# Scaling by the gates on VectorE and ScalarE, a unit's logits formed together, and another order of the first loads, in a fused attention and mixture-of-experts kernel

## The chip, the cores and the metric

One core of one Trainium2 chip runs the whole program. A time is the device time of one execution in microseconds (us). Five executions of the kernel before gave a median of 724.09 us (722.45 to 726.24). The engines are named as in the profile: PE is TensorE (PEld its weight loads), DVE is VectorE, ACT is ScalarE, POOL is GpSimd, SP is SyncE, which issues transfers here. A "q" behind a name (SPq, POOLq) is that engine's own queue of instructions.

## The reference

Sliding-window causal attention over 8 batches, 8 heads, 576 positions and a head size of 64 comes first, then a mixture of experts in which each of the 4608 tokens goes to one of eight experts. Both are f32.

```python
# attention: q, k, v of (8, 8, 576, 64), window 64
scores = scale * np.matmul(q, k.transpose(0, 1, 3, 2))
mask = (rel >= 0) & (rel < window)
scores = np.where(mask, scores, -1000000000.0)
scores = scores - np.max(scores, axis=-1, keepdims=True)
attn = np.exp(scores)
attn = attn / (np.sum(attn, axis=-1, keepdims=True) + 1e-09)
x = (attn @ v)            # laid out as (4608, 512)
# experts: w_gate (512, 8), w1 (8, 512, 1024), w2 (8, 1024, 512)
logits = x @ w_gate
expert_idx = np.argmax(logits, axis=1)
probs = np.exp(logits - logits.max(-1, keepdims=True))
probs /= probs.sum(-1, keepdims=True) + 1e-09
gate_w = probs[np.arange(N), expert_idx]
h = np.maximum(x_sorted[lo:hi] @ w1[e], 0.0)     # for each expert e
y_sorted[lo:hi] = h @ w2[e]
return gate_w[:, None] * y
```

The kernel multiplies x by its gate before the experts and not y after them, which is the same since the gate is positive.

## The kernel before, in words

**Units and steps.** Attention is cut into 16 units: four groups of two batches (`bg`), and in each group four pairs of heads (`g`). A unit is three steps (`c` = 0, 1, 2), so there are 48 steps, numbered `s`; each covers three blocks of 128 tokens. `step(s)` (lines 941 to 971) writes out one turn of a pipeline by hand, and every engine runs its own instructions strictly in that order. In step `s` these things are issued, in this order:

1. `scored(s + 1)`: 24 matmuls (line 628); `masked`, six DVE instructions that add the mask and take the row maximum (line 641); `softened`, six exponentials on ACT (line 651).
2. `weighted(s - 1)`: 24 matmuls with v (line 674) into the one bank 6.
3. `logit(s - 3)`: the matmuls with the gate's weights (line 711) from the transposed x of step `s - 3`.
4. `flipped(s)`: six PE transposes of the probabilities (line 659) into two banks of PSUM, copied out by DVE (first head) and ACT (second head), line 661.
5. `divided(s - 1)`: three DVE instructions (lines 684, 685, 688) that normalise and write x into a tile `xs`.
6. in the first step of a unit, the loads of v two units ahead and of q and k three units ahead, all on SP's queue; v also needs six POOL copies a unit (lines 567, 569, 573), which make a second, shifted copy `vb` of it.
7. `turned(s + 3)`: PE transposes of q and k for the next unit (eight, line 595, in the first two steps of a unit, two, line 587, in the third) and ACT copies.
8. `x_turned(s - 2)`: three PE transposes of x (line 699) and an ACT copy `xT` (line 702).
9. whatever `todo` holds for this step.

Steps 4, 7 and 8 and the small work of the routing take their PSUM banks in turn from one ring of four (`tr_ring`, banks 2 to 5). A step with all five uses comes back to its first bank with `x_turned`: those transposes wait until DVE has copied the first head of `flipped` out of that bank.

**Routing.** When the logits of a block of three tiles of a group are complete, `by_tokens` copies them out (ACT, line 722), transposes them in the next step (PE, line 725) and copies them back (DVE, line 726). After the third, `choose(bg)` works out expert, gate and rank in five parts, mostly small DVE instructions (lines 742 to 798). `after(s, ...)` (lines 878 to 900) spreads the parts over the following steps, then, tile by tile for nine tiles, `place` (two bf16 DVE instructions, line 802, that build the one-hot rows `lo`), `weigh` (x times its gate, 128x512 f32, in place) and `store` (the DMA of `xs` to `x_dram`, on POOL's queue). The groups' routing starts at steps 15, 27 and 39; the fourth group is dealt with after the last step. For groups 0 and 1 all nine `weigh` are on POOL (line 813). For group 2 seven are on POOL and two on ACT (line 811). In step 45 `first_tiles` forms `hi_e` on DVE (line 907) from the ranks, multiplies it with `lo` on PE (54 matmuls, line 914), and gathers the first tokens of expert 0. The matmuls of the experts follow from about 214 us.

**The first loads.** Before step -3 one queue, SP's, gets: q and k of unit 0 (eight DMAs of 128 KB), the gate's weights, a row of zeros for `x_dram`, the last 64 positions of q, k and v (six DMAs), v of unit 0 (four), q and k of unit 1 (eight), v of unit 1 (four), q and k of unit 2 (eight). A DMA further waits until the eighth DMA before it has landed, since eight semaphores go round.

Of the kernel before, what the change touches and what calls it, by code (L numbers as in the profile page):

```python
# [11 lines left out]
F32 = mybir.dt.float32  # L12
# [24 lines left out]
def kernel(  # L37
# [10 lines left out]
    nc = tc.nc  # L48
# [447 lines left out]
    with tc.manual_schedule(), ExitStack() as held, ExitStack() as brief:  # L496
# [2 lines left out]
        rp = held.enter_context(tc.tile_pool(name="rp", bufs=2))  # L499
        att = brief.enter_context(tc.tile_pool(name="att", bufs=2))  # L500
        xp = brief.enter_context(tc.tile_pool(name="xp", bufs=3))
        sc_ring, tr_ring = cycle((0, 1)), cycle((2, 3, 4, 5))


# [32 lines left out]
        def load_qk(u):  # L537
            bg, g = units[u]
            qks[u] = [qk_m(((u % 3 + 2) % 3 * 2 + n) * 1024, BG, NV, 2, D) for n in range(2)]
            for i in range(BG):  # L540
                for t, src in zip(qks[u], (q, k)):
                    for h in range(2):
                        nc.sync.dma_start(
                            out=t[:, i, :, h, :],
                            in_=src[bg * BG + i, 2 * g + h, 0:SM, :].rearrange("(p j) d -> p j d", j=NV),
                        )

        def load_rests(bg):

            at = 6144 + bg % 2 * 2048  # L550
            vr = qk_m(at + 1024, BG, H, D)
            rests[bg] = [qk_m(at, H, D), qk_m(at + 512, H, D), vr]
            for t, src in zip(rests[bg], (q, k)):
                for i in range(BG):
                    nc.sync.dma_start(
                        out=t[i * D : (i + 1) * D], in_=src[bg * BG + i, :, SM:S, :].rearrange("h p d -> p h d")
                    )
            for i in range(BG):
                nc.sync.dma_start(out=vr[D:P, i], in_=v[bg * BG + i, :, SM:S, :].rearrange("h p d -> p h d"))

        def load_v(u):
            bg, g = units[u]
            va, vb = v_ring[u % NVR]
            for i in range(BG):
                for h in range(2):
                    nc.sync.dma_start(out=va[:, i, :, h, 0:D], in_=whole(v, u, i, h))
                G.tensor_copy(out=vb[D:P, i, NV - 1, :, 0:D], in_=rests[bg][2][D:P, i, 2 * g : 2 * g + 2])

                nc.gpsimd.tensor_copy(  # L569
                    out=vb[0:D, i].rearrange("p j h d -> p (j h d)"),  # L570
                    in_=va[D:P, i].rearrange("p j h d -> p (j h d)"),
                )
# [141 lines left out]
                )  # L714
            return g == NG - 1

        def by_tokens(bg, c):

            if c == 0:
                logits_of[bg] = rp.tile([P, NTB, E], F32, name="logits")  # L720
            lgT = rp.tile([ST * GE, P], F32, name="lgT")
            nc.scalar.copy(out=lgT[:], in_=lgs[bg][:, c, :])
            yield
            tr = banks[next(tr_ring)](0, ST, P)
            nc.tensor.transpose(out=tr[:, 0, 0 : ST * GE], in_=lgT[:], identity=ident[0 : ST * GE, 0 : ST * GE])
            V.tensor_copy(
                out=logits_of[bg][:, c * ST : (c + 1) * ST, :],
                in_=tr[:, 0, 0 : ST * GE].rearrange("p (m e) -> p m e", e=GE)[:, :, 0:E],
            )

        last = B // BG - 1
# [187 lines left out]

        N = NU * NST  # L920
        load_qk(0)
        nc.sync.dma_start(out=wg[:, :, 0:E], in_=moe_w_gate.rearrange("(g p) e -> p g e", p=P))
        nc.sync.dma_start(out=x_dram[NT : NT + 1, :], in_=zrow[:])
        load_rests(0)
        load_v(0)
        load_qk(1)
        load_v(1)
        load_qk(2)

        for g in range(NG):  # L930
            step = NST * (g // 2) + g % 2 + 1
# [9 lines left out]
        def step(s):  # L941
            if 0 <= s + 1 < N:
                prs[s + 1] = softened(*masked(s + 1, scored(s + 1)))
            if 0 <= s - 1 < N:
                px = weighted(s - 1, pTs.pop(s - 1))
            ripe = 0 <= s - 3 < N and logit(s - 3)
            if 0 <= s < N:
                pTs[s] = flipped(prs.pop(s))
            if 0 <= s - 1 < N:
                divided(s - 1, px)  # L950
            if s >= 0 and s % NST == 0:
                u = s // NST
# [12 lines left out]
            if ripe:  # L965
                bg, c = (s - 3) // (NG * NST), (s - 3) % NST
                parts = by_tokens(bg, c)
                next(parts)
                todo.setdefault(s + 1, []).append(partial(next, parts, None))
                if c == NST - 1:  # L970
                    after(s + 1, choose(bg), bg)


        for n, s in enumerate((N - 6, N - 3)):
# [79 lines left out]
    with tc.manual_schedule():  # L1054
# [36 lines left out]

        def any_number():

            tiles_of = rt.tile([P, E, NTILE], F32, name="tiles_of")
            V.tensor_tensor(
                out=tiles_of[:], in0=_inner(cum[:], NTILE), in1=_ins(lane[:, 0:NTILE], 1, E), op=ALU.is_le
            )
            with nc.allow_low_precision("integers"):
                V.tensor_reduce(out=expert_i[:], in_=tiles_of[:].rearrange("p e t -> p t e"), axis=AX.X, op=ALU.add)
# [60 lines left out]
```

## Time and profile before

| | |
|---|---|
| median of five runs | 724.09 us (722.45 to 726.24) |
| the profiled execution: its own time | 719.12 us |
| its span | 717.4 us |
| its granted TensorE clock | 0.992 |
| PE, DVE, ACT, POOL busy | 687.2, 495.9, 258.6, 350.1 us |
| steps -3 to 47 and what follows to the first expert matmuls | 0 to about 215 us |
| `weigh` on POOL, 25 instructions | median 1562 ns |
| `weigh` on ACT, 11 instructions | median 708 ns |

The page has an overview, a list of groups of instructions with what ended the idle time before them, and further views: the timeline lists single instructions with start, duration and, in brackets, idle time before them and what ended it; the table of windows gives busy time per engine in stretches of the span. PE's busy time is modelled from pipelined matmuls, so a stretch in which PE is busy throughout can still be a slow one: the duration of a known bundle of matmuls tells which.

### The profile page before, as it was taken

The page shows a single profiled execution, that of the slowest core. Times are in us where ns is not written, and L with a number is a line of the kernel's source. Part 1 is how long each engine was busy: PE and PEld are TensorE (multiplying, and loading weights), DVE is VectorE, ACT ScalarE, POOL GpSimd, SP SyncE. Part 2 cuts the span into 40 slices and gives each one's busy share as a digit, 9 for nine tenths or more (in the row PEclk, how much of TensorE's full clock was granted, in tenths as well). Part 3 has the DMA queues.
Part 4 walks back from the last instruction along what each step waited for, and adds up shares of the span by engine and source line. Part 5 has one row for each costly group of instructions (what it writes and reads, how often), then busy time and mean ns, then how long its engine had stood idle before and what let it go on. Part 6 is the DMA issues. An engine that isn't in the chain of part 4 may idle for free. (4 is left out here: it accounts for less than half of the span.)

```text
span 717.4 us, 17946 instructions
## 1 busy us (share of the span) xinstructions
PE 687.2 (96%) x6882; PEld 605.8 (84%) x6882; DVE 495.9 (69%) x1636; ACT 258.6 (36%) x653; POOL 350.1 (49%) x360
## 2 busy tenths in 40 slices
PE   5999999999979999999999999999999999999993
PEld 3787888888769897897999999899889799889993
DVE  3576898898956768676776677568756677766731
ACT  4788888888745112101121111122110112111110
POOL 4223748569574117757452446645265745272001
PEclk9999999999999999999999999999999999999997
DMA  8998988989443364617102620640451710111000
GB/s 157 214 208 180 185 176 230 210 182 246 146 136 114 102 241 145 199 59 276 53 16 66 216 101 32 208 146 2 139 196 59 275 52 18 61 37 61 2 31 28
DMA packets 137288, 93.37 MB, mean 130 GB/s; under 512 B 117008, under 2 KB 117008, under 8 KB 137170
## 3 DMA queue, kind: packets, MB, share of 16 engines
q1 hardware_dynamic: 127858, 62.16, 32.5%
q0 software_dynamic: 8736, 27.53, 11.9%
q10 hardware_dynamic: 576, 2.10, 0.9%
q8 instruction: 74, 1.21, 0.7%
q14 instruction: 44, 0.36, 0.2%
HBM read 72.89 MB, written 20.45 MB: 130 GB/s over the span
## 5 line engine op out<-in xcount | busy, mean ns | idle before, releaser
L315 DVE STREAM_TRANSPOSE v_m<-qk_m 32x256 f32<-32x256 f32 x304 | 132.3, 435 | 7.9 <-DMA qk_m<-x_dram,at_g 2.3
L344 PE MATMUL bank<-qk_m,s 128*128 128x128 f32 x1024 | 122.5, 275 | 0.1
L344 PEld LDWEIGHTS bank<-qk_m,s 128*128 128x128 f32 x1024 | 118.3, 192 | 0.3 <-issue 0.3
L275 POOL DMA_INDIRECT qk_m<-x_dram,at_g x38 | 41.0, 1078 | 141.1 <-DVE v_m L315 112.7
L651 ACT ACTIVATE pr<-pr,mx 128x128 f32<-128x128 f32 x288 | 89.7, 390 | 32.6 <-DVE mx L641 32.3
L344 PE MATMUL bank<-qk_m,w 128*128 128x128 f32 x768 | 93.8, 275 | 0.7 <-PEq L1077 0.7
L344 PEld LDWEIGHTS bank<-qk_m,w 128*128 128x128 f32 x768 | 90.6, 192 | 4.2 <-issue 3.9
L295 POOL DMA_INDIRECT out_dram<-v_m,at_s x42 | 42.4, 1010 | 87.4 <-DVE v_m L384 85.2
L641 DVE CUSTOM_DVE_ANT_0 pr<-bank,mask 128x128 f32<-128x128 f32 x288 | 64.4, 286 | 29.0 <-PE bank L628 27.6
L384 DVE TENSOR_TENSOR v_m<-bank,v_m 128x256 f32<-128x256 f32 (+1 forms) x95 | 43.8, 480 | 44.9 <-PE bank L388 30.1
L569 POOL COPY v_m<-v_m 64x520 f32<-64x520 f32 x32 | 19.8, 619 | 69.1 <-DMA v_m<-in_v_dram 59.8
L140 POOL TENSOR_TENSOR s<-w 128x1024 f32<-128x1024 f32 x22 | 52.2, 2373 | 0.0
L674 PEld LDWEIGHTS bank<-v_m,pT 128*64 128x64 f32 x1152 | 40.8, 140 | 11.5 <-DVE xs L688 5.4
L674 PE MATMUL bank<-v_m,pT 128*64 128x65 f32 x1152 | 47.5, 230 | 2.5 <-DVE xs L688 2.4
L351 ACT COPY qk_m<-bank 128x512 f32<-128x512 f32 x16 | 9.4, 587 | 108.4 <-PE bank L344 70.2
L388 PE MATMUL bank<-qkT_m,v_m 128*128 128x256 f32 x216 | 48.3, 379 | 0.0
L628 PE MATMUL bank<-qkT_m 64*64 64x128 f32 x1152 | 45.6, 290 | 0.1
L388 PEld LDWEIGHTS bank<-qkT_m,v_m 128*128 128x128 f32 x216 | 41.0, 190 | 5.5
L595 PE MATMUL bank<-ident,qk_m 128*128 128x128 f32 x256 | 36.8, 287 | 8.3 <-DMA qk_m<-in_q_dram 7.5
L444 PEld LDWEIGHTS bank<-qk_m,w 128*128 128x128 f32 x320 | 43.9, 190 | 0.9 <-issue 0.7
L444 PE MATMUL bank<-qk_m,w 128*128 128x160 f32 x320 | 44.4, 299 | 0.4 <-ACT qk_m L327 0.4
L327 ACT COPY qk_m<-v_m 128x512 f32<-128x512 f32 x38 | 21.6, 615 | 58.6 <-DVE v_m L315 58.6
(174 smaller groups left out, 1248.0 us busy)
## 6 DMA issues: line engine op xcount, KB each, us to landing
w<-in_moe_w_dram SPq DMA_DIRECT2D x11, 2048.0 KB, 9.9
qk_m<-in_q_dram SPq DMA_DIRECT2D x72, 128.0 KB, 4.0
qk_m<-in_k_dram SPq DMA_DIRECT2D x72, 128.0 KB, 3.7
v_m<-in_v_dram SPq DMA_DIRECT2D x64, 128.0 KB, 4.2
qk_m<-in_moe_w_dram SPq DMA_DIRECT2D x3, 2048.0 KB, 10.9
x_dram<-xs POOLq DMA_DIRECT2D x6, 512.0 KB, 4.8
x_dram<-xs POOLq DMA_DIRECT2D x3, 768.0 KB, 5.1
w<-in_moe_w_dram ACTq DMA_DIRECT2D x4, 512.0 KB, 4.4
```

Of the source, the lines that this page charges most:

```text
L140: op()
L275: G.indirect_dma_start(out=xg[c], out_offset=None, in_=x_dram[:, :], in_offset=bass.IndirectOffsetOnAxis(ap=at_g[:, c : c + 1], axis=0),)
L295: put = G.indirect_dma_start(out=out[:, :], out_offset=bass.IndirectOffsetOnAxis(ap=at_s[:, c : c + 1], axis=0), in_=ys[c], in_offset=None ...
L315: V.transpose(out=xn[b * QD : (b + 1) * QD, :, :, a * QD : (a + 1) * QD].rearrange("p c g i -> p (c g) i"), in_=rows[a * QD : (a + 1) * QD ...
L344: nc.tensor.matmul(acc[:, f, :], lhsT=a[:, g, f * P : (f + 1) * P], rhs=b[:, g, :], start=(first and f == 0 and g == 0), stop=(g == HG - 1 ...
L384: plus = lambda out, a, b: V.tensor_tensor(out=out, in0=a, in1=b, op=ALU.add)
L388: nc.tensor.matmul(acc, lhsT=a[:, f, :], rhs=b[:, f, :], start=(start and f == 0), stop=(stop and f == HF - 1), skip_group_check=True,)
L444: nc.tensor.matmul(acc[:, i], lhsT=w1[:, g, f * P : (f + 1) * P], rhs=xq[:, g].rearrange("p c s -> p (c s)")[:, 0:HALF], start=(i + g == 0 ...
L628: nc.tensor.matmul(out_, lhsT=qT[rows, t, a * WINDOW : (a + 1) * WINDOW], rhs=rhs, start=True, stop=True, skip_group_check=True,)
L641: V.tensor_tensor_reduce(out=prs[h][:, m, :], in0=scs[h][:, m, :], in1=mask[:, m0 + m, :], scale=-scale, scalar=-2 * MASKED, op0=ALU.add, ...
L651: nc.scalar.activation(out=y, in_=y, func=AF.Exp, scale=-1.0, bias=mx[:, h, m : m + 1])
L674: nc.tensor.matmul(px[a * D : (a + 1) * D, h, m, :], lhsT=pTs[h][:, m, a * D : (a + 1) * D], rhs=vt[:, h, :], start=True, stop=True, skip_ ...
```

## The change

`weigh` leaves POOL. Groups 0 and 1 do all nine on DVE, one a step, at steps 4 to 12 after the routing's start; their `place` goes from 5 + 2m/3 to 5 + m, one a step. Group 2 does tiles 0, 1, 3 and 6 on ACT and five on DVE, some a step later than before. Stores stay on POOL's queue and follow the `weigh` of each third tile.

`logit` is called for all three steps of a unit at once, in the unit's third step, and `by_tokens` then moves three blocks in one ACT copy, three transposes into one bank, and one DVE copy. The fourth group keeps the form with single blocks.

Of the first loads, k of unit 0 and k's last positions go to ACT's queue. q and k of unit 1 come ahead of v of units 0 and 1; the gate's weights come behind these, the row of zeros last. A small buffer in a branch that these inputs don't take moves into another tile.

```diff
@@ load_qk / load_rests
-                for t, src in zip(qks[u], (q, k)):
+                for t, src, queue in zip(qks[u], (q, k), (nc.sync, nc.sync if u else nc.scalar)):
                     for h in range(2):
-                        nc.sync.dma_start(
+                        queue.dma_start(
...
-            for t, src in zip(rests[bg], (q, k)):
+            for t, src, queue in zip(rests[bg], (q, k), (nc.sync, nc.sync if bg else nc.scalar)):
@@ by_tokens
-        def by_tokens(bg, c):
+        def by_tokens(bg, c, n=1):
...
-            lgT = rp.tile([ST * GE, P], F32, name="lgT")
-            nc.scalar.copy(out=lgT[:], in_=lgs[bg][:, c, :])
+            lgT = (rp if n == 1 else lt).tile([ST * GE, n, P], F32, name=f"lgT{n}")
+            nc.scalar.copy(out=lgT[:], in_=lgs[bg][:, c : c + n, :])
             yield
-            tr = banks[next(tr_ring)](0, ST, P)
-            nc.tensor.transpose(out=tr[:, 0, 0 : ST * GE], in_=lgT[:], identity=ident[0 : ST * GE, 0 : ST * GE])
+            tr = banks[next(tr_ring)](0, n, ST * GE)
+            for i in range(n):
+                nc.tensor.transpose(out=tr[:, i], in_=lgT[:, i], identity=ident[0 : ST * GE, 0 : ST * GE])
@@ after
-                    do(5 + m * 2 // 3, partial(place, bg * NTB + m))
-                    do(5 + m * 2 // 3, partial(weigh, bg, m, G))
+                    do(5 + m, partial(place, bg * NTB + m))
+                    do(4 + m, partial(weigh, bg, m, V))
                     if m % ST == ST - 1:
-                        do(5 + m * 2 // 3, partial(store, bg, m // ST, G))
+                        do(4 + m, partial(store, bg, m // ST, G))
...
-                do((2, 2, 3, 3, 4, 4, 4, 5, 5)[m], partial(weigh, bg, m, nc.scalar if m in (2, 6) else G))
+                do((2, 3, 3, 4, 4, 4, 5, 5, 5)[m], partial(weigh, bg, m, nc.scalar if m in (0, 1, 3, 6) else V))
@@ first loads
         load_qk(0)
+        load_rests(0)
+        load_qk(1)
+        load_v(0)
+        load_v(1)
         nc.sync.dma_start(out=wg[:, :, 0:E], in_=moe_w_gate.rearrange("(g p) e -> p g e", p=P))
+        load_qk(2)
         nc.sync.dma_start(out=x_dram[NT : NT + 1, :], in_=zrow[:])
-        load_rests(0)
-        load_v(0)
-        load_qk(1)
-        load_v(1)
-        load_qk(2)
@@ step
-            ripe = 0 <= s - 3 < N and logit(s - 3)
+            ripe = 0 <= s - 3 < N and s % NST == NST - 1 and [logit(n) for n in range(s - 5, s - 2)][-1]
```

More of the change, by code (lines that the diff above doesn't have):

```diff
@@ L501 @@
         xp = brief.enter_context(tc.tile_pool(name="xp", bufs=3))
+        lt = brief.enter_context(tc.tile_pool(name="lt", bufs=1))
         sc_ring, tr_ring = cycle((0, 1)), cycle((2, 3, 4, 5))
@@ L552, in load_rests @@
             rests[bg] = [qk_m(at, H, D), qk_m(at + 512, H, D), vr]
-            for t, src in zip(rests[bg], (q, k)):
+            for t, src, queue in zip(rests[bg], (q, k), (nc.sync, nc.sync if bg else nc.scalar)):
                 for i in range(BG):
-                    nc.sync.dma_start(
+                    queue.dma_start(
                         out=t[i * D : (i + 1) * D], in_=src[bg * BG + i, :, SM:S, :].rearrange("h p d -> p h d")
@@ L715, in logit @@
             return g == NG - 1
-        def by_tokens(bg, c):
+        def by_tokens(bg, c, n=1):
             if c == 0:
                 logits_of[bg] = rp.tile([P, NTB, E], F32, name="logits")
-            lgT = rp.tile([ST * GE, P], F32, name="lgT")
-            nc.scalar.copy(out=lgT[:], in_=lgs[bg][:, c, :])
+            lgT = (rp if n == 1 else lt).tile([ST * GE, n, P], F32, name=f"lgT{n}")
+            nc.scalar.copy(out=lgT[:], in_=lgs[bg][:, c : c + n, :])
             yield
-            tr = banks[next(tr_ring)](0, ST, P)
-            nc.tensor.transpose(out=tr[:, 0, 0 : ST * GE], in_=lgT[:], identity=ident[0 : ST * GE, 0 : ST * GE])
+            tr = banks[next(tr_ring)](0, n, ST * GE)
+            for i in range(n):
+                nc.tensor.transpose(out=tr[:, i], in_=lgT[:, i], identity=ident[0 : ST * GE, 0 : ST * GE])
             V.tensor_copy(
-                out=logits_of[bg][:, c * ST : (c + 1) * ST, :],
-                in_=tr[:, 0, 0 : ST * GE].rearrange("p (m e) -> p m e", e=GE)[:, :, 0:E],
+                out=logits_of[bg][:, c * ST : (c + n) * ST, :],
+                in_=tr.rearrange("p n me -> p (n me)").rearrange("p (m e) -> p m e", e=GE)[:, :, 0:E],
             )
@@ L965, in step @@
             if ripe:
-                bg, c = (s - 3) // (NG * NST), (s - 3) % NST
-                parts = by_tokens(bg, c)
+                bg = (s - 3) // (NG * NST)
+                parts = by_tokens(bg, 0, NST)
                 next(parts)
                 todo.setdefault(s + 1, []).append(partial(next, parts, None))
-                if c == NST - 1:
-                    after(s + 1, choose(bg), bg)
+                after(s + 1, choose(bg), bg)
         for n, s in enumerate((N - 6, N - 3)):
@@ L1092, in any_number @@
         def any_number():
-            tiles_of = rt.tile([P, E, NTILE], F32, name="tiles_of")
+            tiles_of = v_m(2080, E, NTILE)
             V.tensor_tensor(
-                out=tiles_of[:], in0=_inner(cum[:], NTILE), in1=_ins(lane[:, 0:NTILE], 1, E), op=ALU.is_le
+                out=tiles_of, in0=_inner(cum[:], NTILE), in1=_ins(lane[:, 0:NTILE], 1, E), op=ALU.is_le
             )
             with nc.allow_low_precision("integers"):
-                V.tensor_reduce(out=expert_i[:], in_=tiles_of[:].rearrange("p e t -> p t e"), axis=AX.X, op=ALU.add)
+                V.tensor_reduce(out=expert_i[:], in_=tiles_of.rearrange("p e t -> p t e"), axis=AX.X, op=ALU.add)
             _, (tiles,) = nc.values_load_multi_w_load_instructions(
```

## The prediction, made before the result was known

> **What bounds the kernel now.** I read the page's overview, then the windows, then PE's timeline step by step, then all engines where PE stands.
>
> ```profile
> PE 687.2 (96%) x6882; PEld 605.8 (84%) x6882; DVE 495.9 (69%) x1636; ACT 258.6 (36%) x653; POOL 350.1 (49%) x360
> ...
> 0.00:10.00 10.00, 4.39 (x20) 2.98 (x24) 2.29 (x14) 3.05 (x5) 6.65 (x29) 1.00 0.56 122
> 10.00:20.00 10.00, 6.69 (x62) 4.75 (x63) 3.18 (x25) 5.40 (x16) 3.12 (x7) 1.00 1.10 197
> ...
> 80.00:90.00 10.00, 10.00 (x198) 8.37 (x195) 9.52 (x50) 8.50 (x26) 5.60 (x9) 1.00 0.91 172
> 190.00:200.00 10.00, 9.40 (x159) 7.61 (x154) 9.86 (x46) 7.63 (x22) 8.70 (x8) 1.00 0.73 254
> 200.00:210.00 10.00, 6.42 (x122) 5.37 (x122) 5.74 (x36) 5.32 (x16) 6.32 (x8) 0.83 0.38 116
> ```
>
> PE is the bound overall. In a window's row the columns are stretch, length, busy PE, PEld, DVE, ACT, POOL, then granted clock, DMA share, GB/s. PE has room at the start (8.9 us of 20 idle) and near 200 us; between these DVE is nearly as full as PE, and POOL is not.
>
> ```profile
> 4.69 1.09 PE L595 MATMUL bank<-ident,qk_m 128*128 128x128 f32 x4 [4.69 <-DMA qk_m<-in_q_dram]
> ...
> 13.47 0.45 PE L587 MATMUL bank<-ident,qk_m 128*128 128x128 f32 x1 [1.18 <-DMA qk_m<-in_k_dram]
> ...
> 18.52 2.26 PE L595 MATMUL bank<-ident,qk_m 128*128 128x128 f32 x8 [1.64 <-DMA qk_m<-in_q_dram]
> 20.71 1.56 PE L628 MATMUL bank<-qkT_m 64*64 64x128 f32 x24
> ...
> 25.15 0.89 PE L628 MATMUL bank<-qkT_m 64*64 64x128 f32 x24
> ```
>
> PE waits for the first loads, and it is slow until about 23.2 us: 24 score matmuls take 1.56 us at 20.71 and 0.89 at 25.15, though the granted clock shows 1.00 for both. It turned fast 4.6 us after its last wait (18.52); at 207.4, 4.4 us after another.
>
> In steady state a step lasts 4.07, 4.07 and 3.41 us through a unit. What exceeds that in steps 19 to 38 I add up from the starts of line 628: 1.0 us, without the routing's own matmuls. From step 39 on:
>
> ```profile
> 187.98 0.55 PE L699 MATMUL bank<-ident,xs 128*128 128x128 f32 x3 [1.42 <-DVE pT L661]
> 192.69 0.30 DVE L802 TENSOR_SCALAR lo<-lane,low,tok_a 128x128 bf16<-128x128 bf16 x1
> 192.91 0.80 DVE L802 TENSOR_SCALAR lo<-lane,low,tok_b 128x128 bf16<-128x128 bf16 x1
> ...
> 202.67 0.27 DVE L907 TENSOR_TENSOR hi_e<-key,hi_id 128x108 bf16<-128x108 bf16 x1
> 203.00 1.52 PE L914 MATMUL bank<-hi_e,lo 128*128 128x4 bf16 x54 [2.70 <-DVE hi_e L907]
> ```
>
> PE stands for DVE: 1.42 us in step 42 after ten routing instructions in a row, 2.70 us in step 45. In the timeline DVE has no gap over 0.45 us from 174.76 (step 39's start is 170.50) to `hi_e`'s end at 202.94. So DVE sets the end of this stretch. POOL's last `weigh` starts at 199.7 and nothing on PE waits for it; it does slow `place`: consecutive instructions start 0.22 us apart when POOL rests, and up to 0.62 beside its `weigh`.
>
> **The change part by part.** The sum is against the profiled execution, span 717.4, time 719.12; the median shown is 5.0 above it, and I add this at the end. A measurement here tells about 0.3%, 2.2 us, from no change.
>
> *First loads.* Each DMA is 0.131 MB and SP starts one per 0.65 us, about 197 GB/s, near what the DMA engines moved at share 1.1. Counting 0.21 MB a us from 2.5 us on, when the first bytes must be moving for q's two DMAs to be there at 4.69: k of unit 1's first batch is the 18th DMA, there at 2.5 + 18 x 0.131 / 0.21 = 13.7 us, against some 19 now; v of unit 0's first batch is the 24th, at 17.5. PE's transposes start at 4.7 as before and run without the waits to about 9.2, the score of step 0 follows 0.6 us earlier than at 9.88, step 1's at about 11.5, the flip when ACT has its exponentials (about 12), unit 1's transposes at 13.7. ACT now issues six DMAs (0.65 each, the last two after a first one has landed) and only then loads its table (1.28 us): its first copy moves from 5.81 to about 7, still ahead of the score at 9.2 that needs it. So PE reaches v (line 674) at 15.5 to 16.6, and v is what is late next: the first batch at 17.5, then POOL's 0.62 and 0.51 us for `vb`, so 18.6 instead of no wait. From there to step 2's start are most of line 674, the flip and eight transposes: 0.9 + 0.87 + 1.04 at the fast rate, step 2 at 21.4; or 1.45 + 1.5 + 2.1 at the slow one, 23.6; now 25.15. The gain is 3.75 or 1.55, the ends of this price; a loss is excluded because every DMA that PE or POOL needs before step 2 starts earlier or within 1.5 us of its old place and PE comes 6 us later than that now. PE will have been busy for 10 us, but stands 2 to 3 us at v; after the 2.70 us at 200.3 it was slow (1.56 at 204.44), after 1.42 at 187.98 fast (0.89). I take the middle, 2.7, and 0.4 of the 0.97 us for which step 9 waits for unit 4 at 55 us, as SP is ahead by then: **-3.1**. The gate's weights (behind v) are first used in step 5, some 10 us after they land; the row of zeros is not read until the experts.
>
> [...]
>
> *Logits together.* 288 matmul rows as before; nine per unit (1.05 us) now stand in the third step ahead of the flip, and none in the others: steps become 3.72, 3.72, 4.11, the same sum. Six ACT copies of 0.26 and six DVE copies of 0.19 go; they are hidden by PE in steps 13 to 38, so nothing. But PE's x transposes come 0.35 earlier in the first two steps (3.30 after a step's start, not 3.65), and DVE must have freed their bank by then.
>
> *Weigh on DVE, groups 0 and 1.* Price of one: the trace has no f32 128x512 instruction of this kind from SBUF. Below it lies `place` (start to start 0.22, a quarter of the elements), above it the f32 sums of line 140 (0.69 long, so 0.60 start to start, as other rows start 0.09 before the last ends). A 128x128 cast from f32 (line 182) takes 0.23, where line 641 and the two-input rows, 1.08 ns an element, would give 0.28: half the slope for one input. 0.144 + 512 x 0.00054 = 0.42, less 0.09, plus 0.07 for a scalar read from SBUF (`place`, with two, is that much dearer): I take **0.40**, nearest the cast, ends 0.22 and 0.60.
> Behind it wait line 641 of the next step, then the copy of line 661, then PE's x transposes. In a unit's third step the copy starts at 3.42 and `divided` ends 1.43 later, 0.74 into the next step. Then place 0.45, weigh 0.40, six of line 641 1.27, the copy to the transposes 0.60: 3.46, against 3.30. That is 0.16 us in steps 21, 24, 27, 33, 36, and I add 0.15 each for POOL's copies of v (2.8 us a unit), beside which `place` took up to 0.7. In step 28 the routing of group 1 (logit copy and four instructions, 1.35) meets the last `place` and `weigh` of group 0, now two steps later than before: about 1.0. Sum 2.5, less the 1.0 of now, in which POOL's `weigh` slowed `place`: **+1.5**. Without a `weigh` a step has 0.4 to 0.6 us to spare.
> Stores wait on POOL for DVE; behind them are copies of v, three steps ahead of use. The tile of the last store of use (group 1, step 36) is written again in step 39, 11 us later, against 0.75 to issue and 4.6 to land: nothing.
>
> *Group 2, steps 38 to 45.* All on DVE's chain, no cover. Added: six `weigh` (one of group 1's, five of group 2's) 2.4; two `place` of group 1, which ended before step 38, 0.9; a wait for the later flip in step 41 0.4; the later start of the chain in step 39 0.2. Gone: contention, as 18 `place` of steps 42 to 44 took 5.9 from start to start and would take 18 x 0.22 = 4.0, 1.9 less. **+2.1**, ends +1.0 (weigh at 0.22) and +3.3 (0.60). ACT's two more `weigh`, 0.71 each, are hidden: ACT waits for DVE here. The first gather waits for the last store, issued about when it is now plus this shift; its rows land some 3 us before PE turns them at 214.
>
> Sum: -3.1 + 1.5 + 2.1 = **+0.5**: span 717.9, time 719.6, as a median **724.6**: no change to be told.
>
> **The rivals.** *A, faster: DVE has room.* If a `weigh` costs what a `place` costs, 0.22, the third-step chain is 3.28, under 3.30: the middle is -0.3, the end +1.0; and with PE still fast at v the start is -4.15. Sum -3.5: 720.6. For it: the halved slope of the cast; against: four times the elements.
> *B, slower: DVE is the new bound.* At 0.60 a `weigh`, the five steps lose 0.51 each, step 28 1.3: +2.85; the end +3.3; start -3.1: +3.05, 727.1. It decides from about 0.53. For it: the rows of line 140; against: these have two inputs.
> *C: v behind unit 1 is the new wait* and PE is slow again after it: the start gives 1.55 and nothing at step 9: +2.05, 726.1.
> *D: the loads are bound by the DMA engines, not by their order*: shares of 0.9 to 1.3 up to 48 us and the wait of 0.97 us at 55 say that PE catches up with the DMAs whatever it gained. Then the start is worth 0.5: +3.1, 727.2. Against: 58 to 200 us show no such wait, so SP gets ahead.
>
> **How the numbers follow.** The forecast 0.38 (722.3 to 726.6), A 0.27 (719 to 722), B 0.17, C 0.10, D 0.08. Faster by over 0.3% (below 721.9): A and 0.05 of the forecast, 0.32. Slower (above 726.3): B, D, half of C and 0.03 of the forecast, 0.33. Within: 0.35. The range from 719.5, A's sum with its end term at nothing, to 728.5, B with C's start.
>
> **What would show it.** Step 2's first score at 21 to 24 us, with PE's wait at line 674 for POOL or v; eight transposes of unit 1 near 14; DVE rows of `weigh` starting 0.40 before the next; `place` 0.22 apart in steps 42 to 44; step starts 3.72, 3.72, 4.11 apart with 0.1 to 0.4 more where group 0 and 1 are weighed and 1 at step 28; from step 39's start to `hi_e` 34.5 us instead of 32.4. It is wrong if `weigh` blocks on POOL's copies, if PE does not wait for bank or flip as I have it, or if the first loads share one issuer.

## The result

The changed kernel takes 724.78 us (median of 47 executions, 721.57 to 728.67), the kernel before 722.27 (89 executions, 719.25 to 727.01): ratio 1.0027, 95% interval 1.0018 to 1.0037, so about 2.0 us slower (1.3 to 2.7). The means, 724.66 and 722.69, have this ratio too; the medians lie 2.5 us apart. The forecast was 724.6 and "no change to be told". The number came out as said, but partly by luck: it is 0.5 us above a median of five executions, 724.09, and the median of 89 lies 1.8 us lower. The change is small and still clear of no change. Several of the forecast's terms did not come out.

The two profiled executions differ by more than the medians: span 722.1 (its own time 723.78) against 717.4. Part of that is chance: from step 46's start to the end, which the change hardly touches, before's profile took 512.95 us, the shortest of the 14 profiles of this study (the others 513.4 to 517.0, the changed kernel's 514.5).

| stretch | before | after | difference | forecast |
|---|---|---|---|---|
| 0 to start of step 12 | 64.51 | 66.18 | +1.67 | -3.1 |
| step 12 to 19 | 27.58 | 28.00 | +0.42 | 0 |
| step 19 to 39 | 78.41 | 77.36 | -1.05 | +1.5 |
| step 39 to 46 | 33.94 | 36.05 | +2.11 | +2.1 |
| step 46 to the end | 512.95 | 514.47 | +1.52 | 0 |

### The profile page after: what moved, and what is told of

The parts are those of the page before. It is cut to its first block, busy times and chain, and to the rows that moved or that the text cites. A ratio compares the mean times of both kernels' runs of the same rounds, so it can differ in the third digit from the quotient of the medians.

```text
span 722.1 us, 17934 instructions
## 1 busy us (share of the span) xinstructions
PE 685.7 (95%) x6882; PEld 609.5 (84%) x6882; DVE 499.2 (69%) x1653; ACT 260.2 (36%) x649; POOL 311.3 (43%) x335
## 3 DMA queue, kind: packets, MB, share of 16 engines
HBM read 72.89 MB, written 20.45 MB: 129 GB/s over the span
## 5 line engine op out<-in xcount | busy, mean ns | idle before, releaser
L629 PE MATMUL bank<-qkT_m 64*64 64x128 f32 x1152 | 45.6, 289 | 0.3 <-DVE mx L642 0.3
L660 PE MATMUL bank<-ident,pr 128*128 128x128 f32 x288 | 43.8, 290 | 0.0
```

The source lines that it names most:

```text
L629: nc.tensor.matmul(out_, lhsT=qT[rows, t, a * WINDOW : (a + 1) * WINDOW], rhs=rhs, start=True, stop=True, skip_group_check=True,)
L660: nc.tensor.transpose(out=tr[:, m, :], in_=prs[h][:, m, :], identity=ident[:])
```

## The profile after

The overview of the changed kernel and its table of windows (stretch, length, busy PE, PEld, DVE, ACT, POOL, granted clock, DMA share, GB/s):

```profile
PE 685.7 (95%) x6882; PEld 609.5 (84%) x6882; DVE 499.2 (69%) x1653; ACT 260.2 (36%) x649; POOL 311.3 (43%) x335
...
0.00:10.00 10.00, 3.29 (x15) 2.95 (x16) 2.27 (x14) 2.69 (x4) 6.75 (x29) 1.00 0.93 160
10.00:20.00 10.00, 8.89 (x99) 6.52 (x97) 4.53 (x37) 7.28 (x22) 1.05 (x3) 1.00 1.36 205
50.00:60.00 10.00, 7.62 (x99) 6.24 (x92) 4.13 (x29) 5.32 (x16) 3.49 (x8) 0.72 0.83 186
190.00:200.00 10.00, 8.59 (x157) 7.17 (x161) 9.86 (x55) 9.28 (x26) 2.04 (x3) 1.00 0.47 143
```

POOL's 39 us of `weigh` are gone, and DVE, whose `weigh` takes 12.7 us in all, shows only 3.3 us more than before: `place`, no longer beside POOL's `weigh`, takes 22.6 us in all and took 29.1. PE works 12.2 of the first 20 us, not 11.1: the new loads do fill the start. But a hole has come between 50 and 60, where PE was busy for 9.03 us before, at a granted clock of 1.00. PE's timeline of the changed kernel (start, duration, in brackets the idle time and what ended it):

```profile
5.91 1.94 PE L596 MATMUL bank<-ident,qk_m 128*128 128x128 f32 x8 [5.91 <-POOL mask L518]
...
18.58 0.30 PE L675 MATMUL bank<-v_m,pT 128*64 128x65 f32 x2
19.16 0.45 PE L675 MATMUL bank<-v_m,pT 128*64 128x65 f32 x6 [0.28 <-DMA v_m<-in_v_dram]
20.41 0.73 PE L675 MATMUL bank<-v_m,pT 128*64 128x65 f32 x16 [0.80 <-POOL v_m L574]
...
22.75 0.89 PE L629 MATMUL bank<-qkT_m 64*64 64x128 f32 x24
...
53.39 0.63 PE L596 MATMUL bank<-ident,qk_m 128*128 128x128 f32 x4 [1.50 <-DMA qk_m<-in_q_dram]
54.90 1.09 PE L596 MATMUL bank<-ident,qk_m 128*128 128x128 f32 x4 [0.88 <-DMA qk_m<-in_k_dram]
...
56.55 1.56 PE L629 MATMUL bank<-qkT_m 64*64 64x128 f32 x24
```

The first row names POOL's mask as what ended the wait. What came last is q's second DMA: it lands at 5.78 us in the trace.

Step 2 starts at 22.75, not 25.15, with v and its POOL copies as the wait that comes last, and PE stays fast there. The lead of 2.4 us lasts to step 9 (49.29 against 51.61). There PE waits 2.4 us for unit 4's q and k, then runs slow (the score bundle takes 1.56, not 0.89), and by step 12 it is 1.67 us behind. In the kernel before the same two waits came to 0.97 us, and PE stayed fast:

```profile
55.10 0.63 PE L595 MATMUL bank<-ident,qk_m 128*128 128x128 f32 x4 [0.56 <-DMA qk_m<-in_q_dram]
56.14 0.63 PE L595 MATMUL bank<-ident,qk_m 128*128 128x128 f32 x4 [0.41 <-DMA qk_m<-in_k_dram]
```

DVE's timeline and PE's, late in attention:

```profile
196.99 0.48 DVE L815 TENSOR_SCALAR xs<-xs,gate 128x512 f32<-128x512 f32 x1
197.39 0.31 DVE L804 TENSOR_SCALAR lo<-lane,low,tok_a 128x128 bf16<-128x128 bf16 x1
197.62 0.31 DVE L804 TENSOR_SCALAR lo<-lane,low,tok_b 128x128 bf16<-128x128 bf16 x1
...
205.82 0.27 DVE L909 TENSOR_TENSOR hi_e<-key,hi_id 128x108 bf16<-128x108 bf16 x1
```

```profile
191.00 0.55 PE L700 MATMUL bank<-ident,xs 128*128 128x128 f32 x3 [1.76 <-DVE pT L662]
...
206.15 1.51 PE L916 MATMUL bank<-hi_e,lo 128*128 128x4 bf16 x54 [3.05 <-DVE hi_e L909]
```

The next instruction starts 0.40 us after a `weigh`, `place` goes at 0.22 to 0.23, and PE's waits for DVE grow from 1.42 and 2.70 to 1.76 and 3.05.

## Experiments: the parts alone

Each ratio is to the kernel before on the same chip, with a 95% interval; 0.1% is 0.72 us. Differences between two runs are worked out from the ratios, their intervals by adding half widths in squares.

| kernel | us | ratio to before |
|---|---|---|
| the whole change | 724.78 | 1.0027 (1.0018 to 1.0037) |
| loads alone | 721.97 | 0.9992 (0.9973 to 1.0011) |
| logits alone | 721.64 | 0.9990 (0.9969 to 1.0011) |
| weigh alone | 724.69 | 1.0052 (1.0030 to 1.0074) |
| all but the loads | 725.42 | 1.0055 (1.0031 to 1.0078) |
| change, w1 later, sums later | 725.70 | 1.0056 (1.0034 to 1.0077) |
| change, group 2 as before | 723.71 | 1.0023 (1.0002 to 1.0045) |
| logits, loads, w1 later, sums later | 721.79 | 1.0011 (0.9986 to 1.0035) |
| all but the loads, stores earlier | 724.18 | 1.0030 (1.0010 to 1.0051) |
| change, stores earlier | 723.20 | 1.0005 (0.9987 to 1.0023) |
| logits, loads, w1 later, sums ahead | 724.60 | 1.0026 (1.0006 to 1.0047) |
| change, stores earlier, group 2 as before | 723.07 | 1.0004 (0.9985 to 1.0024) |
| the last, w1 later, sums ahead | 726.09 | 1.0056 (1.0031 to 1.0080) |

**The first loads alone.** To the kernel before:

```diff
         load_qk(0)
-        nc.sync.dma_start(out=wg[:, :, 0:E], ...)
-        nc.sync.dma_start(out=x_dram[NT : NT + 1, :], in_=zrow[:])
         load_rests(0)
-        load_v(0)
         load_qk(1)
+        load_v(0)
         load_v(1)
+        nc.sync.dma_start(out=wg[:, :, 0:E], ...)
         load_qk(2)
+        nc.sync.dma_start(out=x_dram[NT : NT + 1, :], in_=zrow[:])
```

(and k of unit 0 and k's last positions on ACT's queue)

> Only the first loads are changed (k of unit 0 on ACT's queue, q and k of unit 1 ahead of v). Theory: the start is paced by the transfers, so what step 2 gains (2.4 us earlier in the trace of the change) is given back where PE waits for unit 4's q and k in step 9 (some 53 to 55 us) and is slow after it: 0 to +2 us, PE in step 12 not before its old 64.5. Rival, the forecast's own term: the gain is kept, -2.5 to -3.5 us, step 12 at 61 to 62.

0.9992: no gain that can be told. Step 1 starts at 16.29 (20.71 before), but PE then waits for v (1.35 and 0.80 us) and is slow again (the last 16 matmuls of line 674 take 1.19 us, in the changed kernel 0.73), so that step 2 starts at 25.24 (25.15): rival C in this execution. Over all profiles there are two kinds of start. Of nine with the new loads, four have step 2 at 22.75 to 23.00, with PE fast, and five at 24.25 to 26.17: four of these are slow after v, and the one at 24.25 stayed fast but waited 3.0 us in sum at v. The five with the old loads have 24.60 to 26.05. So on the mean over the profiles the new loads bring step 2 forward by 0.9 us (24.24 against 25.15), not by the 2.4 of the changed kernel's own profile.

**The logits alone.** `by_tokens` and `logit` as in the changed kernel, all else as before:

```diff
-            ripe = 0 <= s - 3 < N and logit(s - 3)
+            ripe = 0 <= s - 3 < N and s % NST == NST - 1 and [logit(n) for n in range(s - 5, s - 2)][-1]
```

> Only the logits of a unit are formed together. Theory: nine logit matmuls in a row take 0.79 us from start to start of what follows, three bundles of three 3 x 0.35 = 1.05; a unit is 0.26 shorter, over some 14 units that PE bounds -3 to -4 us. Rival, as the forecast had it: the matmuls are the same, so 0 (-0.5 to +0.5), or a little worse as the x transposes come earlier against DVE's copy.

0.9990: not told from no change (-0.7 us, plus or minus 1.5), and the 3 to 4 us of the theory are not there. But the bundle is cheaper than its three parts. PE's timeline of the changed kernel, a bundle of logits and what follows it:

```profile
88.24 0.86 PE L712 MATMUL bank<-xT,wg 128*32 128x128 f32 x18
89.03 0.87 PE L660 MATMUL bank<-ident,pr 128*128 128x128 f32 x6
```

The next bundle starts 0.79 us later, where three separate ones took 3 x 0.35 = 1.05. Undisturbed steps are 3.72, 3.72, 3.85, so a unit is 0.26 us shorter. Alone, this loses its lead to step 9's wait (step 10 at 57.00 against 57.02); of the 2.3 us for the nine units from step 12 to 39 (105.07 against 105.99) 0.9 is left.

**The products alone.** `after` as in the changed kernel, all else as before:

```diff
-                    do(5 + m * 2 // 3, partial(place, bg * NTB + m))
-                    do(5 + m * 2 // 3, partial(weigh, bg, m, G))
+                    do(5 + m, partial(place, bg * NTB + m))
+                    do(4 + m, partial(weigh, bg, m, V))
...
-                        do(5 + m * 2 // 3, partial(store, bg, m // ST, G))
+                        do(4 + m, partial(store, bg, m // ST, G))
```

(and group 2's nine)

> Only the scaling by the gates moves to VectorE and ScalarE, with its new steps. Theory, as the forecast had it: VectorE sets the end of steps 39 to 45, and they grow by about 2; the steps before lose up to 1: +2 to +3.5 us, hi_e 34 to 35 us after step 39's start instead of 32.4. Rival: freed from GpSimd, VectorE has room for the scaling: -1 to +0.5 us, and the cost of the whole change comes from the loads alone.

1.0052: this part makes the change slower, by 3.8 us (2.2 to 5.3). The tail, from step 39's start to `hi_e`'s end, takes 33.57 us, under the 34 to 35 expected. In the profile one step stands out: step 28 takes 9.18 us (4.18 before).

```profile
123.45 1.54 POOL L822 DMA_DIRECT2D x_dram<-xs  x2
...
129.69 0.56 DVE L688 TENSOR_TENSOR xs<-bank,rec 128x384 f32<-128x384 f32 x1 [3.41 <-DMA x_dram<-xs]
...
130.30 1.62 PE L674 MATMUL bank<-v_m,pT 128*64 128x65 f32 x24 [2.35 <-DVE xs L688]
```

These are lines of POOL, DVE and PE in order of time. A `divided` (of step 27's program on DVE) writes into a tile whose store has not landed; PE's step 28 waits 2.35 us for it and is slow after it (1.62 instead of 0.97). It is the tile of group 0's second store. That store has moved from step 23 to step 24, and was issued at 123.45, in before's profile at 120.45, where the same write did not wait:

```profile
120.45 1.35 POOL L822 DMA_DIRECT2D x_dram<-xs  x2
127.28 0.56 DVE L688 TENSOR_TENSOR xs<-bank,rec 128x384 f32<-128x384 f32 x1
```

**All but the loads.** The changed kernel with the first loads as before:

> The change without its first loads (logits together and scaling moved). Theory: logits -3 to -4 and scaling +2 to +3.5 add up: -2 to +0.5 us, so 1.5 to 3.5 below the whole change, as the loads do harm. Rival, the forecast's terms: without a gain of 3.1 at the start it is 3.6 slower than before.

1.0055, 4.0 us slower than before, as the rival had it. So the loads are worth 0.28% (plus or minus 0.25), 2.0 us, beside the other two parts, which is more than they gave alone. The same wait is there:

```profile
122.14 0.62 POOL L570 COPY v_m<-v_m 64x520 f32<-64x520 f32 x1 [7.15 <-DMA v_m<-in_v_dram]
...
124.42 0.51 POOL L574 COPY v_m<-v_m 64x390 f32<-64x390 f32 x1
...
124.87 1.54 POOL L824 DMA_DIRECT2D x_dram<-xs  x2
...
130.72 0.56 DVE L689 TENSOR_TENSOR xs<-bank,rec 128x384 f32<-128x384 f32 x1 [3.10 <-DMA x_dram<-xs]
```

Step 24 is the first of a unit: six copies of v are put on POOL's queue ahead of what `todo` holds. POOL waits 7.15 us for that v here, and the store, whose last `weigh` ended at 117.5, stands behind the copies until 124.87. In the changed kernel's own profile v came 4 us sooner, the store went out at 120.90, and no divide waited. So whether this wait comes depends on when v arrives.

## Experiments: the wait for the stores

**Stores one step earlier, without the loads.** The products that a store follows move with it. To the kernel of the last run:

```diff
-                    do(4 + m, partial(weigh, bg, m, V))
+                    do(3 + m, partial(weigh, bg, m, V))
                     if m % ST == ST - 1:
-                        do(4 + m, partial(store, bg, m // ST, G))
+                        do(3 + m, partial(store, bg, m // ST, G))
```

> The logits together and all products moved, the first loads as before (725.4 us, with a stall of some 3 us in step 28), and here the products and stores of groups 0 and 1 one step earlier (place stays). The stores are so issued by POOL ahead of the step's copies of v, not behind them. Theory (the stall is the divide of step 28 waiting for a store that stands on POOL's queue behind copies waiting for v): no wait of the divide on x_dram, step 28 under 5 us (7.22), time 721 to 723. Rival (the stall is DVE's own load, for which the store is only the last name): step 28 stays at 6 us or more, or the steps before lose as much, time 724.5 to 726.

The wait is gone, the store's two DMAs go out at 114.71 and 115.72, and step 28 takes 3.83 us instead of 7.22:

```profile
114.71 0.83 POOL L824 DMA_DIRECT2D x_dram<-xs  x1
```

The ratio fell from 1.0055 to 1.0030, 1.8 us (plus or minus 2.2), at the low end of the theory; in absolute time, 724.18, the number missed the 721 to 723 expected.

**The whole change with these stores.**

> The whole change, with the products and stores of groups 0 and 1 one step earlier, so that POOL issues a store ahead of the step's copies of v. In the changed kernel's profile no divide waited for a store; in the profile of the kernel that differs from it only in group 2's products one did, for 3.87 us of DVE, 2.65 of PE. Theory (that wait comes in a part of the executions of the changed kernel, and its median holds a part of it): ratio to before 0.999 to 1.001 (1.0027 with the change), no wait of a divide on x_dram. Rival (the median of the changed kernel is without it): ratio 1.002 to 1.004.

1.0005 against 1.0027: 1.6 us (plus or minus 1.5), as the theory had it; the low end of the rival, 1.002, is still inside the interval. The two pairs together give 1.7 us (plus or minus 1.2). Counted over the profiles: of the five kernels with the late stores three show the wait on `x_dram` (3.41, 3.10 and 3.87 us on DVE), of the four with the early ones none. The changed kernel's own profile is one of the two without, which is why two traces alone don't show it.

## Experiments: group 2 and the tail

**Group 2 as before**, in the changed kernel:

```diff
-                do((2, 3, 3, 4, 4, 4, 5, 5, 5)[m], partial(weigh, bg, m, nc.scalar if m in (0, 1, 3, 6) else V))
+                do((2, 2, 3, 3, 4, 4, 4, 5, 5)[m], partial(weigh, bg, m, nc.scalar if m in (2, 6) else G))
```

> The changed kernel, with group 2's nine products by POOL and ACT in their old steps; groups 0 and 1 stay on DVE. Theory (group 2's products lengthen DVE's chain of the tail by the predicted 2.1 us): from step 39's start to the end of hi_e 32.4 to 33.0 us (34.55 in the changed kernel, 32.44 before), step 46 and all behind it about 2 us earlier, time 722.4 to 723.2. Rival (the tail is set by PE or by the stores and gathers, and DVE's shorter chain gives nothing): hi_e 1 to 2 us earlier but the experts start no earlier, time 724.3 to 725.3.

1.0023 against 1.0027: nothing that can be told (0.3 us, plus or minus 1.7). The profile has 34.11 us from step 39 to `hi_e`'s end, not 32.4; this part of the theory fails. It also has the store's wait (step 28 of 8.91 us), which may have hidden a gain.

**Group 2 as before, with the early stores**, so that this wait is out of the way:

> As the whole change with the earlier stores, and group 2's nine products by POOL and ACT in their old steps. Theory (group 2 on DVE costs the tail the predicted 2.1 us, and the wait for the store hid that in the run that changed group 2 alone): 1.5 to 2.5 us below the run with only the earlier stores, from step 39's start to hi_e about 33 us. Rival (the tail's length follows from other things, as it also was 34.2 to 35.4 us in runs with the old products): within 0.7 us of it.

1.0004 against 1.0005 (plus or minus 0.0027, or 1.9 us), with 35.03 us in the tail, as the rival had it. The two tests together give 0.2 us (plus or minus 1.3), which leaves no room for the 1.5 to 2.5 expected. The length from step 39's start to `hi_e`'s end in all 14 profiles:

| products | us |
|---|---|
| all as before (5 kernels) | 32.44, 32.45, 33.63, 35.42, 32.85: mean 33.4 |
| groups 0, 1 moved, group 2 as before (3) | 34.11, 35.03, 33.82: mean 34.3 |
| all moved (6) | 34.55, 33.57, 33.99, 34.01, 34.18, 34.55: mean 34.1 |

On the mean the tail is 0.8 us longer in the nine kernels with moved products, which is less than the spread of the five others, and it isn't shorter where group 2 is as before. One step does tell them apart: step 39 takes 4.01 or 4.02 us in the three kernels with the logits together and all products as before, and 4.56 to 4.94 in the eight in which groups 0 and 1 have moved as well, whether group 2 has or not.

## Experiments: w1 and the sums of it

Step 9's wait ends the lead of the loads. ACT's queue starts four loads of w1 (512 KB each, for the first expert) in steps 1 to 5, and POOL forms four sums of them (`L966`).

**w1 later, in the changed kernel:**

```diff
-            step = NST * (g // 2) + g % 2 + 1
+            step = (2, 5, 10, 12)[g]
...
-            todo.setdefault(3 * NST + n, []).append(op)
+            todo.setdefault(13 + n, []).append(op)
```

> The changed kernel, with the four quarter loads of w1 on ACT's queue in steps 2, 5, 10 and 12 (were 1, 2, 4 and 5) and POOL's sums of them in steps 13 to 16 (were 9 to 12). Theory (the loads of w1 crowd unit 4's q and k out of the DMA engines): the waits before unit 4's transposes in step 9 (1.50 and 0.88 us in the changed kernel's profile) go or fall below 0.5 us, PE stays fast, step 12 starts near 63 us (66.18 in the changed kernel), and the time is 2 to 3.5 us below the changed kernel's 724.8: 721 to 723. Rival (the DMA engines are the bound up to step 9 whatever the order, the prediction's rival D): the waits only move to later units, steps 12 to 18 are reached no earlier than in the changed kernel, time 724 to 726. A cost to be looked for in both: the sums now stand beside other routing work of DVE than before.

The first half came true in this profile: no wait at step 9, step 12 at 62.89 (66.18). The time did not: 725.70, ratio 1.0056. The lead is lost in steps 20 and 21, which take 7.42 and 6.53 us. POOL, DVE and PE there, in order of time:

```profile
96.32 2.38 POOL L966 TENSOR_TENSOR s<-w 128x1024 f32<-128x1024 f32 x1
96.51 2.22 DVE L800 CAST low<-r_half 128x9 f32<-128x9 int32 x1
...
98.64 2.64 DVE L815 TENSOR_SCALAR xs<-xs,gate 128x512 f32<-128x512 f32 x1
98.66 2.33 POOL L966 TENSOR_TENSOR s<-w,s 128x1024 f32<-128x1024 f32 x1
...
101.96 2.18 PE L629 MATMUL bank<-qkT_m 64*64 64x128 f32 x24 [3.49 <-DVE mx L642]
```

A cast of nine columns, 0.17 us elsewhere, and a `weigh`, 0.48, end with the POOL sum beside them. PE idles 3.49 us and is slow after it (2.18 instead of 0.89).

**Logits, loads and w1 later, products as before:**

> The kernel before, with the logits together, the new first loads and the spread loads of w1; all products as before. Theory (the start's gain of 2.4 us at step 2 is lost only to the loads of w1, and the logits together gain 0.26 us a unit): step 12 near 62 to 63 us (64.51 before), step 39 near 167.5 to 169 (170.50 before), time 719.5 to 721, under the 722.2 of before. Rival (the gains before step 9 are always eaten by the DMA engines): step 12 at 64.5, time 721.3 to 722, as the logits alone gave.

SP now issues unit 4's q at 45.38, where the changed kernel, with the same loads before it, issues it at 49.54. Step 12 starts at 60.24 (64.51 before), step 39 at 168.15 (170.50), better than expected. The time, 721.79 and 1.0011, is not: 2.7 us of the lead go in steps 20 and 21 beside the sums, and the tail takes 35.42 us, where PE waits 1.42 us and is slow for a step (its score bundle takes 1.48).

**The same with the sums ahead of step 12's copies of v:**

```diff
-            step = (2, 5, 10, 12)[g]
+            step = (2, 5, 10, 11)[g]
...
-            todo.setdefault(13 + n, []).append(op)
+            todo.setdefault(3 * NST + 2, []).append(op)
```

> The kernel before, with the logits together, the new first loads, w1's quarter loads in steps 2, 5, 10 and 11, and all four of POOL's sums of them at the end of step 11, ahead of the copies of v of step 12 on POOL's queue; all products as before. In the run with the sums in steps 13 to 16 they stood beside routing instructions and products of DVE, which then took as long as the sum beside them, and steps 20 to 22 lost 5 us of the 4.1 gained. Theory (the sums at about 67 to 77 us meet no routing): step 21 starts near 95.5 us (99.63 before), time 718 to 720, ratio 0.994 to 0.997. Rival (whatever is gained in front is given back, by DMA or in the last steps, where DVE sets the end): ratio 0.998 to 1.002.

1.0026, where 0.994 to 0.997 was expected. Step 9 lasts 5.32 us here: PE waits 1.2 us for unit 4, though w1's loads up to then stand as in the last run. Step 16 starts at 77.06 (80.45 before), so a lead of 3.4 us is there; step 16 then takes 8.28 us. The sums were expected at 67 to 77 us, but the copies of v ahead of them on POOL's queue ended only at 72.8. At 72.89 to 82.32 us they do meet routing instructions:

```profile
77.66 2.36 POOL L966 TENSOR_TENSOR s<-w 128x1024 f32<-128x1024 f32 x1
77.76 2.35 DVE L747 TENSOR_TENSOR r_top<-logits,r_mx 128x72 f32<-128x72 f32 x1
...
79.98 2.34 POOL L966 TENSOR_TENSOR s<-w,s 128x1024 f32<-128x1024 f32 x1
80.14 2.27 DVE L748 TENSOR_TENSOR r_top<-r_top,e_m 128x72 f32<-128x72 f32 x1
```

Two DVE instructions of 0.28 and 0.23 us take 4.6, and PE waits 3.99. In the kernel before the same two stand at 81.04 and 81.36, in a gap of six copies of v between the third sum (to 80.06) and the fourth:

```profile
81.04 0.28 DVE L745 TENSOR_TENSOR r_top<-logits,r_mx 128x72 f32<-128x72 f32 x1
83.28 2.37 POOL L964 TENSOR_TENSOR s<-w,s 128x1024 f32<-128x1024 f32 x1
```

With the four sums in a row there is no such gap. The changed kernel, whose steps come later, misses it in part: `r_top` takes 1.40 us at 82.20 beside the fourth sum, and step 16 5.03 instead of 4.07.

**All that was mended at once:** this kernel with groups 0 and 1 on DVE and the early stores.

> The logits together, the new first loads, w1 loaded and summed as in the run before this one, group 2's products as before; groups 0 and 1 weighed by DVE, with the earlier stores. It differs from the kernel with the old products throughout only in groups 0 and 1. Theory (DVE's products cost what the prediction gave, 1.5 us): 1 to 2 us above that kernel, ratio 0.996 to 0.999. Rival (DVE has no room at all for them: 11 products of 0.40 us or more on the path and each stalls PE): 3 us or more above it. Second rival (they cost nothing, as POOL's products slowed DVE by as much): within 0.5 us of it.

1.0056 against 1.0026: groups 0 and 1 cost 0.30% (plus or minus 0.32), 2.2 us. That lies beside the theory's 1 to 2, but the second rival (nothing) is not excluded, nor the first (3 us or more). The expected ratio, below 1, fell with that of the run it rests on: `r_top` takes 1.82 and 2.27 us here, step 16 7.40. At step 9 PE waits 0.8 us in this profile.

So of the four profiles with w1's loads put later, step 9's wait is gone in two, and 1.2 and 0.8 us are left in the other two, against 2.4 us in the changed kernel.

None of these kernels is faster than the one before by more than can be measured.

## Why the prediction was right, and where it was not

**First loads, -3.1: wrong at "0.4 of the 0.97 us for which step 9 waits for unit 4 ... as SP is ahead by then".** The order of events was right: v the new wait, then POOL's 0.6 and 0.5 us for `vb`, step 2 between 21.4 and 23.6 (22.75). "PE's transposes start at 4.7 as before" was not: 5.91. And SP was not ahead. It issued unit 4's q at 49.54 against 49.96 before, though every step was some 2.3 us earlier; q and k arrived late and PE fell slow. The runs with w1's loads put later show that these loads had a part in it: the wait went in two of four profiles and was some half as long or less in the others. The 2.7 for step 2 was too much as well: the changed kernel's profile has 2.4, but the mean over the profiles has 0.9. Measured alone, the term is -0.6 us (plus or minus 1.4), beside the other parts -2.0 (plus or minus 1.8). Rival C, given 0.10, is what happens in four of the nine profiled starts. Rival D describes the changed kernel to step 12, but its "not by their order" goes too far: with w1 in another order most of the wait went.

**Logits together, 0: "the same sum" was wrong.** The three bundles together cost 0.79, not 1.05, and the third step 3.85, not 4.11. In the profiles that is 0.26 us a unit, most of it lost again to waits; in the time -0.7 us (plus or minus 1.5), which is not told from the 0.

**Products of groups 0 and 1, +1.5: price right, one step wrong.** In 17 of 23 rows the next instruction starts 0.40 us after a `weigh`. Five rows beside POOL's copies of v take 0.66 or 0.77, so the sign of being wrong "if `weigh` blocks on POOL's copies" shows in part; the forecast had allowed 0.15 us in each of five steps for these copies. Rivals A (0.22) and B (0.60) fall. Steps 21, 24, 33 and 36 lost 0.14, 0.14, 0.35 and 0.14 us (0.31 each forecast), steps 27 and 28 0.85 and 0.33 (0.31 and 1.0 forecast); some 0.3 and 0.1 of these two are also there with the logits together and the old products. From step 19 to 39 the four kernels with the early stores take 78.53 to 79.08 us, the two with the logits together, the old products and no sums in these steps 77.88 and 77.09: 1.2 us on the mean, near the 1.5, though the changed kernel's own 77.36 shows nothing of it. The wrong step is "Stores wait on POOL for DVE; behind them are copies of v, three steps ahead of use ... nothing". It looked at what stands behind the stores and not at what stands ahead of them: the same step's copies of v, which wait for v's DMA. Only the last store's tile was followed to its next use, 11 us later; the tile of group 0's second store is written again 7.4 us after its issue in the changed kernel, 1.7 us after the store has landed, and in the three profiles with the wait DVE is ready for it after 2.4 to 2.8 us. Moving the stores, with their products, ahead of the copies gave back 1.7 us (plus or minus 1.2), which can be most of the change's 2.0.

**Group 2 and steps 38 to 45, +2.1: right in the profile, not in the mean.** 34.5 us forecast, 34.55 in the changed kernel's profile; but over the profiles the moved products add 0.8, not clear of the spread, and `hi_e` in unmoved kernels ends anywhere from 32.4 to 35.4 us after step 39. Before's profile, from which the forecast counted, lies at the low end. (The "ten routing instructions in a row" ahead of step 42's wait are twelve in its rows, from 183.41 to 186.02.) The tests that returned group 2 alone expected 2 us and found none. That expectation misread the forecast's own working: five products of group 2 cost 5 x 0.40 = 2.0, and the contention of `place` that goes is 1.9, so 0.1. The rest was group 1's delay, of which step 39 shows some 0.55 us, with group 2 moved or not.

**The sum.** +0.5 forecast, +2.0 (1.3 to 2.7) measured. The nearness is partly luck, and that of the forecast's 724.6 to the measured 724.78 more so, since its base, 724.09, was 1.8 us too high. The products were given +3.6 in all and measured +3.8 alone (2.2 to 5.3), but some 1.7 of that is the wait for the stores, which was counted at nothing, and the tail is dearer in the forecast than on the mean. The loads were given 1.1 to 2.5 us too much. And the step times of single profiles carry over to the median only roughly: the spans differ by 4.7 us.

**Left open.** What the loads are worth on the median (the two measurements, -0.6 and -2.0, agree within their errors); why PE falls slow after one wait and not after another; and how far the sums beside the routing slow the changed kernel on the median, since no run took that contact away in it.

## What to carry to other kernels

When work leaves a queue, look at what that queue's next instruction now waits for: a store issued from a queue that also waits for loads goes out when the load arrives, and the tile it reads stays taken (without the new loads POOL waited 7.15 us for v, the store went out at 124.87, and DVE waited 3.10 us for its tile). A lead won in front of a fixed pipeline is worth only what the next shared resource leaves of it. Here it ran into w1's loads at step 9 (PE waited 2.4 us), and once these were moved, into POOL's sums at steps 16 to 21 (3.99 and 3.49 us). And before a gain or loss of 2 us in a trace is explained, look at how far the same stretch varies among profiles of kernels that don't differ there.

## What the runs showed of the hardware that was not expected

**DVE stopped by POOL.** Beside a POOL instruction with two f32 inputs of 1024 columns (2.37 us), DVE's two-input instructions from SBUF (0.28 and 0.23 us) took 2.35 and 2.27, a cast 2.22, a `weigh` 2.64. Each ended within 0.3 us of the POOL instruction beside it. A reduction with one input, at 77.50 in the run with the sums ahead of step 12's copies and beside the sum before, took its usual 0.23. Beside POOL's `weigh` (1.56 us), though, `place` lost only up to 0.4 us in the kernel before, so there DVE was not stopped for the whole instruction. What makes the difference is not shown.

**PE's slow phases.** PE was slow after waits of 1.50 and 0.88 us between 51.89 and 54.90 us in the changed kernel (granted clock 0.72 from 50 to 60 us, score bundle of 1.56), and after 1.42 and 0.24 us in another kernel (`L629` of 1.48); after 1.42 us in the kernel before it stayed fast (0.89), and so it did after 0.28 and 0.80 at v in the changed kernel. So no single length of wait decides in these runs. At v the sum of a step's waits sorts the nine starts: 0.8 to 3.0 us in the five fast ones, 3.2 to 4.2 in the four slow ones. At step 9 of the changed kernel 2.4 us in sum were enough. At v PE fell slow in four of the nine profiled starts, though no single wait there was over 1.9 us. It was slow too after the waits of 3.49 and 3.99 us beside the sums (`L629` of 2.18 and 1.56). The traces don't show why the shorter ones sufficed.

**Two queues at the start.** With q on SP's and k on ACT's queue the first transposes start at 5.91 us, not at 4.69. The bytes moved in the first 10 us rise from 122 to 160 GB/s, while q's second DMA, needed first, lands only at 5.78 us; k's second, needed next, lands at 5.30 (5.92 before). That the one delays the other is likely, but no run tests it alone.
